# Attention scores of two heads as 64-row products on alternating halves of the array, in a fused attention, routing, experts and dense kernel

## The chip, the cores and the metric

The kernel runs on one core of one Trainium2 chip. The metric is the device time of one execution in microseconds (us). A core has TensorE (PE; its weight loads have their own row, PEld), VectorE (DVE), ScalarE (ACT), GpSimd (POOL) and SyncE (SP), which here only issues transfers. Each engine works through its own queue in order, and they wait for one another by semaphores.

## The reference

Three layers in float32. First attention, with 4 batches, 8 heads, 576 positions and 64 channels a head, in which each row keeps only the scores within `tau` of its largest:

```python
scores = scale * np.matmul(q, k.transpose(0, 1, 3, 2))
thresh = np.max(scores, axis=-1, keepdims=True) - tau
scores = np.where(scores >= thresh, scores, -1000000000.0)
scores = scores - np.max(scores, axis=-1, keepdims=True)
attn = np.exp(scores)
attn = attn / (np.sum(attn, axis=-1, keepdims=True) + 1e-09)
return np.matmul(attn, v).astype(np.float32)
```

Its output is laid out as 2304 tokens of 512 channels. Second, a gate with noise picks two of eight experts for each token, and the token's row becomes the weighted sum of the two experts' outputs (512 to 1024, ReLU, back to 512). Third, a dense layer 512 to 2048 with a slope `alpha` for negative values, and back to 512. `w_in` and `w_out` come as float64 words.

## The kernel before, in words

The order of all instructions is written out by hand; nothing reorders them within an engine.

Products that need float32 accuracy are made of float32r parts: a value is copied to float32r (hi, on ScalarE), and the rest (lo) is a subtraction on GpSimd or VectorE. For attention, a pair of heads is loaded by two transfers into raw tiles of a ring of five (`load_part`, L261): queries as 64 rows (channels) by 2 x 576 columns, keys as 128 rows by 1216 columns, in which rows 64 to 127 repeat rows 0 to 63 and the second head's last 64 keys stand twice. `split_hi` (L277, ScalarE) and `split_lo` (L285, GpSimd) put the queries' hi on rows 0 to 63 and their lo on rows 64 to 127, so that one product with 128 rows sums hi and lo of the queries; it is made once with the keys' hi and once with their lo. Sixteen pairs go through six sets of tiles (`NSET`).

The attention loop (L731) runs over 80 units. A unit is one pair of heads for one tile of 128 rows, or, for the last 64 rows of each head (marked "t"), both heads in one tile. 64 units are of the first kind. The first 16 are the four tiles of each of the first four pairs; after that come 8 "t" units, 32 of the first kind, 8 "t", 16 of the first kind. For a unit and each of its heads: `s_mm` (L334) makes the scores, 4 products of 288 columns into a tile of PSUM (`ps_s`, two of them); `d1` (L355, VectorE) negates and scales them into SBUF and takes the row minimum; `d1b` (L365, VectorE) adds `tau`; `a1` (L369, ScalarE) takes the exponential; `d2` (L381, VectorE) masks by the threshold and sums the row. Then `t_mm` (L394) transposes the result in three parts into `ps_t` (three buffers), `a2` (L409) copies each to SBUF on ScalarE, `pv` (L423) multiplies with the values into `ps_v`. In iteration i the scores are those of unit i, the masks those of unit i-1, the transposes those of i-2, the products with the values those of i-3.

When a tile's four pairs are through, the routing of its tokens follows in pieces set into later iterations (`x_stages`, `gating`): transposes back to token rows with a store (`rows`, one `ps_t`), gate logits (`logits`, one), their transpose (`flip`, one), the sum over heads on VectorE (`sum_`), and for groups of up to three tiles the choice of experts and an indirect store into the experts' slots `xg`. Token rows use a ring of five buffers, one of which holds zeros first: `zero_init` (L684) writes them over all 640 slots of each expert in iterations 9, 11, ... 23. From iteration 64 the first expert's weights are split as well (L173 on GpSimd), and from the end of the loop on PE works on the experts and the last layer.

SyncE issues nearly all transfers, in program order, and waits at each for the buffer it needs.

Of the kernel before, what the change touches and what calls it, by code (L numbers as in the profile page):

```python
# [5 lines left out]
FR = mybir.dt.float32r  # L6
# [16 lines left out]
KW = S + 640  # L23
# [9 lines left out]
def emit(tc, qt, kt, v, tau, wg, wn, noise, w1, w2, w_in, w_out, alpha, out):  # L33
    """qt [B,HP,64,2*S] and kt [B,HP,64,KW]: head pairs, channels on rows; the second
    head's keys lie as tail, main, tail. v [B,S,H*D]. noise [128,NT,E], alpha [128,16]."""
# [6 lines left out]
    with (  # L42
# [10 lines left out]
        # Memory is cut by hand: what the experts and the last layer need takes the place of  # L53
        # attention's tiles piece by piece, as each of them is done with.
# [101 lines left out]
        # the first block runs while attention drains, in other places  # L156
# [35 lines left out]
        def mm1(ps, n, wc, x, col):  # L192
            """wc: the chunks of the four row blocks; columns from col."""
# [33 lines left out]
        # ======================= attention and routing =======================  # L227
# [30 lines left out]

        raw_tile = Ring([cut(m_early, KW * i, [KW]) for i in range(5)])

        def load_part(n, part):  # L261
            b, hp = divmod(n, HP)
            raw = raw_tile()
            raws[n, part] = raw
            if part == "q":
# [4 lines left out]
        def pair(n):  # L270
            t = m_pair[n % NSET]
            return [cut(t, 0, [2, S], FR), cut(t, 3584, [4, 64], FR), cut(t, 1152, [KW], FR), cut(t, 2368, [KW], FR)]

        for i in range(NSET):
            pool.memset(f32(pair(i)[1][:, 1:3]), 0.0)

        def split_hi(n, part):  # L277
            raw = raws[n, part]
            sets[n] = pair(n)
            if part == "q":  # L280
                act.copy(sets[n][0][:64].rearrange("p h s -> p (h s)"), raw[:64, :2 * S])
            else:
                act.copy(sets[n][2], raw)

        def split_lo(n, part, eng):  # L285
            raw = raws.pop((n, part))
            if part == "q":
                a, zt = sets[n][:2]
                af = a.rearrange("p h s -> p (h s)")
                eng.tensor_tensor(af[64:], raw[:64, :2 * S], f32(af[:64]), op=OP.subtract)  # L290
                t0 = TAIL if (n // HP) % 2 == 0 else 0
                for h in range(2):
                    eng.tensor_scalar(zt[:, 3 * h], f32(a[:, h, t0:t0 + 64]), 1.0, 1.0, op0=OP.mult, op1=OP.mult)
            else:
                eng.tensor_tensor(sets[n][3], raw, f32(sets[n][2]), op=OP.subtract)  # L295

        def split_part(n, part, eng):
            split_hi(n, part)
            split_lo(n, part, eng)
# [20 lines left out]
        # The first tiles of rows go side by side: the head pairs come in slower than they are used.  # L320
# [10 lines left out]
        def s_mm(i, h):  # L331
            b, c, hp = units[i]
            a, zt, hi, lo = sets[b * HP + hp]
            u = st[i]  # L334
            ps = psum_s()
            u["ps", h] = ps
            heads = [h] if c != "t" else [0, 1]
            for x in range(2):
                k = 0
                for hh in heads:  # L340
# [755 lines left out]
```

## Time and profile before

| | |
|---|---|
| runs, us | 1294.23, 1295.03, 1299.9; median 1295.03 |
| profiled execution, span in us | 1295.7 |
| mean granted TensorE clock in it | 0.978 |
| busy in it | PE 1200.5 us (93%), PEld 1074.6, DVE 668.7, ACT 551.1, POOL 528.8 |
| moved by DMA | 148.34 MB, mean 114 GB/s |

The prediction quotes five views. The *page* groups instructions: line, engine, operation, output<-input, shapes and count, then busy time in us and mean ns of one, then idle time of the engine just before them and what ended it; its list of transfers has line, queue, count and KB each. *Windows* give each engine's busy time with the number of instructions in a stretch, then the granted clock (1.00 is full), the share of time that the DMA engines were busy, and the GB/s moved. The *chain of waits* is the sequence of work that ended last, with start and length in us. The *timeline* has start, length, engine, line, operation and count, with idle time before it in brackets. The view of one *line* has the shortest, median and longest duration in ns, then the first and last start. A matmul's end is modelled and matmuls overlap, so what n in a row take in all says more than n durations.

### The profile page before, as it was taken

To read this page: it belongs to the slowest core of one execution; us is meant where nothing else is said; L and a number is where in the kernel's file an instruction comes from. 1 tells how busy PE (TensorE), PEld (TensorE's weight loads), DVE (VectorE), ACT (ScalarE), POOL (GpSimd) and SP (SyncE) were. 2 spreads that over 40 slices of the span, in tenths; PEclk is the share of its full clock that TensorE was granted. 3 is DMA by queue.
4 is the path that set the end of the run, shared out by engine and by line. 5 is a ranking of instruction groups with operands and counts; after the bars stand their busy time and mean duration, and the time that the engine had idled before them with its cause. 6 is when DMAs were issued, how large, how long until landed. Compare 5 with 4: busy or idle time off the path is not lost.

```text
span 1295.7 us, 21188 instructions
## 1 busy us (share of the span) xinstructions
PE 1200.5 (93%) x8198; PEld 1074.6 (83%) x8198; DVE 668.7 (52%) x1493; ACT 551.1 (43%) x1029; POOL 528.8 (41%) x529
## 2 busy tenths in 40 slices
PE   4787778989888999999999999999999999999996
PEld 4676667878777889899898989899989988998995
DVE  5795679997996333333343533345424423432440
ACT  4674557766773344434444444443212212221220
POOL 3534245356434244444454454438314413432430
PEclk9898989999999999999999999999999999999998
DMA  4245542231414365555455556552101101111100
GB/s 125 67 144 202 195 145 80 85 123 73 130 59 143 127 202 179 183 180 183 175 198 185 181 166 207 181 187 90 35 31 41 42 17 41 42 33 33 42 9 18
DMA packets 63559, 148.34 MB, mean 114 GB/s; under 512 B 9502, under 2 KB 9886, under 8 KB 63454
## 3 DMA queue, kind: packets, MB, share of 16 engines
q1 hardware_dynamic: 57534, 127.75, 30.0%
q0 software_dynamic: 5760, 18.88, 4.4%
q8 instruction: 66, 1.08, 0.3%
q10 hardware_dynamic: 160, 0.31, 0.1%
q14 instruction: 39, 0.32, 0.1%
HBM read 98.68 MB, written 48.23 MB: 113 GB/s over the span
## 4 chain that ended last, share of the span: by engine, by line
PE 74%; DVE 12%; DMA 6%; issue 2%; POOL 2%; ACT 1%; SPq 1%; DVEq 0%; POOLq 0%; ACTq 0%
PE ps_t L197 33%; PE ps_s L215 32%; DMA m_early<-in_kt_dram 5%; DVE m_hh L386 4%; DVE m_tmp L362 3%; DVE sm L367 2%; PE ps_t L403 2%; PE ps_s L349 2%; PE ps_v L438 1%; DMA xg<-m_gate 1%; PE ps_t L186 1%; POOL m_pair L295 1%; PE ps_v L186 1%; PE ps_s L197 1%; DVE m_gate L481 1%
## 5 line engine op out<-in xcount | busy, mean ns | idle before, releaser
L215 PE MATMUL ps_s<-m_pair,m_hh 128*128 128x512 f32 x1032 | 338.4, 395 | 0.0
L197 PE MATMUL ps_t<-m_v,m_pair 128*128 128x256 f32 (+1 forms) x2016 | 290.6, 295 | 0.0
L197 PEld LDWEIGHTS ps_t<-m_v,m_pair 128*128 128x128 f32 x2016 | 275.7, 191 | 1.4 <-DVE m_v L190 0.3
L215 PEld LDWEIGHTS ps_s<-m_pair,m_hh 128*128 128x128 f32 x1032 | 193.9, 188 | 39.9
L967 POOL TENSOR_TENSOR m_gate<-m_tmp,m_hh 128x256 fp32r<-128x256 f32 x144 | 104.8, 739 | 249.3 <-ACT m_hh L966 248.2
L215 PE MATMUL ps_s<-m_pair,m_gate 128*128 128x512 f32 x516 | 201.6, 391 | 0.0
L173 POOL TENSOR_TENSOR m_pair<-m_v,m_pair 128x1024 fp32r<-128x1024 f32 x55 | 134.7, 2450 | 140.5 <-ACT m_pair L170 136.9
L197 PE MATMUL ps_t<-m_v,m_early 128*128 128x256 f32 (+1 forms) x1152 | 174.9, 296 | 1.3 <-ACT m_v L189 0.8
L197 PEld LDWEIGHTS ps_t<-m_v,m_early 128*128 128x128 f32 x1152 | 161.7, 191 | 3.0 <-ACT m_v L189 1.1
L386 DVE SCALAR_TENSOR_TENSOR m_hh<-m_tmp,sm,m_hh 128x576 f32<-128x576 f32 x144 | 146.4, 1047 | 27.1 <-ACT m_hh L373 26.9
L373 ACT ACTIVATE m_hh<-m_tmp,sm 128x576 f32<-128x576 f32 x144 | 112.3, 781 | 67.3 <-DVE m_tmp L362 66.9
L208 DVE SCALAR_TENSOR_TENSOR m_gate<-ps_t,m_hh 128x384 fp32r<-128x384 f32 (+1 forms) x120 | 58.2, 492 | 153.4 <-ACT m_hh L207 153.4
L403 PE MATMUL ps_t<-ident,m_hh 128*128 128x128 f32 x576 | 93.1, 286 | 47.0 <-DVE m_hh L386 20.9
L349 PE MATMUL ps_s<-m_pair 128*128 128x288 f32 x640 | 126.2, 325 | 8.2 <-ACT m_pair L642 6.6
L963 DVE TENSOR_SCALAR m_tmp<-ps_t,alpha_t 128x256 f32<-128x256 f32 x144 | 69.7, 484 | 117.1 <-PE ps_t L197 117.0
L966 ACT CAST m_hh<-m_tmp 128x256 fp32r<-128x256 f32 x144 | 58.2, 406 | 146.5 <-DVE m_tmp L964 146.4
L403 PEld LDWEIGHTS ps_t<-ident,m_hh 128*128 128x128 f32 x576 | 68.3, 145 | 60.5 <-ACT m_hh L373 18.9
L362 DVE TENSOR_SCALAR_CACHE_REDUCE m_tmp<-ps_s 128x576 f32<-128x576 f32 x144 | 108.2, 751 | 11.0 <-PE ps_s L349 9.8
L215 PEld LDWEIGHTS ps_s<-m_pair,m_gate 128*128 128x128 f32 x516 | 97.1, 188 | 18.1
L349 PEld LDWEIGHTS ps_s<-m_pair 128*128 128x128 f32 x640 | 95.5, 200 | 9.0 <-ACT m_pair L642 6.5
L207 ACT ACTIVATE m_hh<-ps_t 128x384 fp32r<-128x384 f32 (+1 forms) x120 | 52.0, 439 | 93.8 <-PE ps_t L197 92.7
L854 POOL TENSOR_TENSOR m_tmp<-m_tmp 128x512 f32<-128x512 f32 x32 | 41.4, 1292 | 77.8 <-DVE m_tmp L851 74.4
(204 smaller groups left out, 1529.1 us busy)
## 6 DMA issues: line engine op xcount, KB each, us to landing
m_v<-in_w_dram SPq DMA_DIRECT2D x64, 512.0 KB
xg<-m_gate SPq DMA_DIRECT2D x8, 1280.0 KB
yg<-m_tmp SPq DMA_DIRECT2D x40, 256.0 KB
m_early<-in_kt_dram SPq DMA_DIRECT2D x15, 608.0 KB
m_tmp<-in_w_in_dram SPq DMA_DIRECT2D x16, 512.0 KB
m_tmp<-in_w_out_dram SPq DMA_DIRECT2D x16, 512.0 KB
m_v<-xg SPq DMA_DIRECT2D x20, 256.0 KB
m_rows<-xg SPq DMA_DIRECT2D x20, 256.0 KB
```

What stands on the lines that cost most here:

```text
L173: eng.tensor_tensor(WL[n], wraw.pop(n), f32(WH[n]), op=OP.subtract)
L197: pe.matmul(ps[:, :n], w[wc[d]][:, col:col + 128], x[xx][:, d, :n], start=(k == 0), stop=(k == 11))
L208: dve.scalar_tensor_tensor(hs[1][:, f * n:f * n + n], ps, 0.0, f32(h), op0=OP.max, op1=OP.subtract)
L215: pe.matmul(ps, a[:, o:o + 128], ww[w][:, c:c + 512], start=(f == 0 and k == 0), stop=(f == nf - 1 and k == 2))
L349: pe.matmul(ps[:, x, :288], lhs, kk[:, o + x * 288:o + x * 288 + 288], start=(k == 0), stop=(k == 2 * len(heads) - 1))
L362: dve.tensor_scalar(u["sp"][:, h].rearrange("p (a b) -> p a b", a=2), ps[:, :, :288], -0.125, None, op0=OP.mult, op1=OP.min, accum_out=u[" ...
L373: act.activation(u["em"][:, h], u["sp"][:, h], AF.Exp, bias=u["sm"][:, h:h + 1], scale=-1.0)
L386: dve.scalar_tensor_tensor(u["em"][:, h], u["sp"][:, h], sm[:, 2 + h:3 + h], u["em"][:, h], op0=OP.is_le, op1=OP.mult, accum_out=acc)
L403: pe.transpose(ps[:, j * 128:j * 128 + 128], emf[:, o + j * 128:o + j * 128 + 128], ident)
L963: dve.tensor_scalar(t_, ps, 0.0, alpha_t[:, f:f + 1], op0=OP.min, op1=OP.mult)
L966: act.copy(h, g_)
L967: pool.tensor_tensor(hl[:, f * 256:f * 256 + 256], g_, f32(h), op=OP.subtract)
```

## The change

The layout that the host makes is another: queries and keys of a pair come as 128 rows, the first head's channels on rows 0 to 63 and the second's on rows 64 to 127, with 576 columns of queries and 640 of keys (the last 64 keys of both heads stand twice, in front and at the end). Hi and lo are separate tiles, split once on 128 rows; the subtraction on GpSimd is in two pieces. The raw tiles are nine, and pairs 2 and 3 are requested before the routing constants.

The scores of a head are the products hi x hi, hi x lo and lo x hi, each on the head's 64 rows of the array, the two heads in turn, each into its own `ps_s`. The product lo x lo, which before was part of the sum, is left out. For "t" units the queries stand in tiles with zeros in the off-diagonal blocks, and the three products have 128 rows. `thresh` does on ScalarE what `d1b` did on VectorE. `zero_init` writes only the last 128 of an expert's 640 slots. In an iteration, the scores of both heads, both minima, both exponentials and the threshold now stand in front, then the masks, then the transposes.

```diff
--- before.py
+++ after.py
-KW = S + 640
+KW = S + S - TAIL
...
-        raw_tile = Ring([cut(m_early, KW * i, [KW]) for i in range(5)])
+        raw_tile = Ring([cut(m_early, KW * i, [KW]) for i in range(9)])
 
         def load_part(n, part):
             b, hp = divmod(n, HP)
             raw = raw_tile()
             raws[n, part] = raw
+            sp.dma_start(raw[:, :S] if part == "q" else raw, (qt if part == "q" else kt)[b, hp])
+
+        def pair(n):
+            c = Cuts(m_pair[n % NSET])
+            return [c([S], FR), c([S], FR), c([KW], FR), c([KW], FR), c([128], FR), c([128], FR)]
...
+        def tail_tile(n):
+            t = sets[n]
+            t0 = TAIL if (n // HP) % 2 == 0 else 0
+            for k in range(2):
+                for h in range(2):
+                    r = slice(h * 64, h * 64 + 64)
+                    pool.tensor_scalar(t[4 + k][r, r], f32(t[k][r, t0:t0 + 64]), 1.0, 1.0, op0=OP.mult, op1=OP.mult)
+
+        def split_hi(n, part):
+            if n not in sets:
+                sets[n] = pair(n)
             if part == "q":
-                sp.dma_start(raw[:64, :2 * S], qt[b, hp])
+                act.copy(sets[n][0], raws[n, part][:, :S])
             else:
-                sp.dma_start(raw, kt[b, hp][None].to_broadcast([2, 64, KW]))
...
+                act.copy(sets[n][2], raws[n, part])
+
+        def split_lo(n, part):
+            raw = raws.pop((n, part))
+            hi, lo = sets[n][:2] if part == "q" else sets[n][2:4]
+            w = S if part == "q" else KW
+            for o in range(0, w, w // 2):
+                c = slice(o, o + w // 2)
+                pool.tensor_tensor(lo[:, c], raw[:, c], f32(hi[:, c]), op=OP.subtract)
             if part == "q":
...
+                tail_tile(n)
...
-        def s_mm(i, h):
+        def s_mm(i):
             b, c, hp = units[i]
-            a, zt, hi, lo = sets[b * HP + hp]
+            qh, ql, kh, kl, zh, zl = sets[b * HP + hp]
             u = st[i]
-            ps = psum_s()
-            u["ps", h] = ps
...
+            for h in range(nh(i)):
+                u["ps", h] = psum_s()
+            q0 = 0 if c == "t" else c * 128 + (64 if b % 2 else 0)
             for x in range(2):
...
+                for k, (q, z, kk) in enumerate(((qh, zh, kh), (qh, zh, kl), (ql, zl, kh))):
+                    for h in range(nh(i)):
+                        r = slice(0, 128) if c == "t" else slice(h * 64, h * 64 + 64)
+                        lhs = z if c == "t" else q[r, q0:q0 + 128]
+                        o = (64 - 64 * h) + x * 288
+                        pe.matmul(u["ps", h][:, x, :288], lhs, kk[r, o:o + 288], start=(k == 0), stop=(k == 2))
...
-        def d1b(i):
+        def thresh(i):
             sm, n = st[i]["sm"], nh(i)
-            dve.tensor_scalar(sm[:, 2:2 + n], sm[:, 0:n], taut, None, op0=OP.add)
+            act.activation(sm[:, 2:2 + n], sm[:, 0:n], AF.Identity, bias=taut)
...
+        for n in (2, 3):
+            load_part(n, "q")
+            load_part(n, "k")
...
-        loads = [(n, p) for _, n, p, _ in sched[5:]]
+        loads = [(n, p) for _, n, p, _ in sched[6:]]
...
         def zero_init(e):
-            sp.dma_start(xg[e * N:e * N + CAP].rearrange("(t p) d -> p t d", p=128),
-                         zero[:, None, :].to_broadcast([128, CAP // 128, DM]))
+            sp.dma_start(xg[e * N + CAP - 128:e * N + CAP], zero)
...
         for i in range(END):
             it = i - DT
             tiles = 0 <= it < NU
+            if i < NU:
+                s_mm(i)
+                for h in range(nh(i)):
+                    d1(i, h)
+                for h in range(nh(i)):
+                    a1(i, h)
+                thresh(i)
+            else:
+                do_fill()
+            if 0 < i <= NU:
+                for h in range(nh(i - 1)):
+                    d2(i - 1, h)
             if tiles:
                 t_mm(it, 0)
                 a2(it, 0)
-            if 0 < i <= NU:
-                if nh(i - 1) == 2:
-                    a1(i - 1, 1)
-                else:
-                    d2(i - 1, 0)
-            if i < NU:
-                s_mm(i, 0)
-                d1(i, 0)
-            else:
-                do_fill()
             for f, a in at.pop((i, 0), []):
                 f(*a)
             if tiles and nh(it) == 2:
                 t_mm(it, 1)
                 a2(it, 1)
-            if 0 < i <= NU and nh(i - 1) == 2:
-                for h in range(2):
-                    d2(i - 1, h)
-            if i < NU:
-                a1(i, 0)
             iv = it - 1
...
-            if i < NU and nh(i) == 2:
-                s_mm(i, 1)
-                d1(i, 1)
-            elif i >= NU:
+            if i >= NU:
                 do_fill()
-            if i < NU:
-                d1b(i)
             for f, a in at.pop((i, 1), []):
                 f(*a)
```

The order moves on every engine. On PE, around the routing piece that makes gate logits (L489 before, L485 in the change), in the middle of the loop; ps_s are scores, ps_t transposes, ps_v products with the values. Before:

```order
L489 MATMUL ps_t<-m_last,m_rows 32x128 x4
L403 MATMUL ps_t<-ident,m_hh 128x128 x4
L349 MATMUL ps_s<-m_pair_74 128x288 x4
L403 MATMUL ps_t<-ident,m_hh 128x128 x4
L438 MATMUL ps_v<-m_tmp,m_v_77 64x128 x8
L440 MATMUL ps_v<-m_tmp,m_v_77 128x128
L405 MATMUL ps_t<-ident,m_hh 128x128
L349 MATMUL ps_s<-m_pair_74 128x288 x4
L496 MATMUL ps_t<-ident,m_rows 128x128
```

In the change, with the logits in the first row:

```order
L485 MATMUL ps_t<-m_tmp,m_rows 32x128 x4
L347 MATMUL ps_s<-m_pair_74 128x288 x12
L399 MATMUL ps_t<-ident,m_hh 128x128 x8
L434 MATMUL ps_v<-m_tmp,m_v_77 64x128 x8
L436 MATMUL ps_v<-m_tmp,m_v_77 128x128
L401 MATMUL ps_t<-ident,m_hh 128x128
L492 MATMUL ps_t<-ident,m_rows 128x128
L347 MATMUL ps_s<-m_pair_75 128x288 x12
```

The two groups of 4 products, which stood before and after the transposes, are one group of 12, and both groups of transposes follow it directly; the routing piece stands last in a unit, behind the third transposes, and right in front of the next scores.

On ScalarE around the copy of such logits (L492 before, L488 in the change; L373 and L369 are the exponentials, L415/L417 and L411/L413 the copies of transposes). Before:

```order
L415 COPY m_tmp<-ps_t 128x512
L373 ACTIVATE m_hh<-m_tmp,sm_133 128x576
L415 COPY m_tmp<-ps_t 128x512
L373 ACTIVATE m_hh<-m_tmp,sm_126 128x576
L417 COPY m_tmp<-ps_t 128x128
L283 CAST m_pair_76<-m_early 128x1216
L492 COPY m_rows<-ps_t 128x128
L415 COPY m_last<-ps_t 128x512
L373 ACTIVATE m_hh<-m_tmp,sm_126 128x576
L415 COPY m_last<-ps_t 128x512
L373 ACTIVATE m_hh<-m_tmp,sm_127 128x576
```

In the change:

```order
L369 ACTIVATE m_hh<-m_tmp,sm_144 128x576 x2
L363 ACTIVATE sm_144<-sm_144,taut 128x2
L411 COPY m_tmp<-ps_t 128x512 x2
L413 COPY m_tmp<-ps_t 128x128
L291 CAST m_pair_76<-m_early 128x640
L488 COPY m_rows<-ps_t 128x128
L369 ACTIVATE m_hh<-m_tmp,sm_145 128x576 x2
L363 ACTIVATE sm_145<-sm_145,taut 128x2
L411 COPY m_last<-ps_t 128x512 x2
L413 COPY m_last<-ps_t 128x128
```

Exponentials and copies took turns; now both exponentials and the threshold (L363) of unit i stand ahead of all copies of unit i-2. The split copies (L281, L283; L291 in the change) keep their place at the end of an iteration, with half the columns.

More of the change, by code (lines that the diff above doesn't have):

```diff
@@ L264, in load_part @@
             raws[n, part] = raw
+            sp.dma_start(raw[:, :S] if part == "q" else raw, (qt if part == "q" else kt)[b, hp])
+        def pair(n):
+            c = Cuts(m_pair[n % NSET])
+            return [c([S], FR), c([S], FR), c([KW], FR), c([KW], FR), c([128], FR), c([128], FR)]
+        for i in range(NSET):
+            for z in pair(i)[4:]:
+                for h in range(2):
+                    pool.memset(f32(z[h * 64:h * 64 + 64, 64 - h * 64:128 - h * 64]), 0.0)
+        def tail_tile(n):
+            t = sets[n]
+            t0 = TAIL if (n // HP) % 2 == 0 else 0
+            for k in range(2):
+                for h in range(2):
+                    r = slice(h * 64, h * 64 + 64)
+                    pool.tensor_scalar(t[4 + k][r, r], f32(t[k][r, t0:t0 + 64]), 1.0, 1.0, op0=OP.mult, op1=OP.mult)
@@ L619, in emit @@
         qr, kr = raw_tile(), raw_tile()
[L620 to L629 removed]
+        first = [(qt[0, 0], qr, sets[0][0], sets[0][1], 0, 256), (kt[0, 0], kr, sets[0][2], sets[0][3], 0, 352),
+                 (kt[0, 0], kr, sets[0][2], sets[0][3], 352, KW), (qt[0, 0], qr, sets[0][0], sets[0][1], 256, S)]
+        for i, (src, dst, _, _, c0, c1) in enumerate(first):
+            (sp, act)[i % 2].dma_start(dst[:, c0:c1], src[:, c0:c1])
         sp.dma_start(taut, bass.AP(tensor=tau.tensor, offset=tau.offset, ap=[[0, 128], [1, 1]]))
@@ L633, in emit @@
         load_v(0)
-        load_part(2, "q")
-        qa, zt0, khi, klo = sets[0]
-        for i, (c0, c1) in enumerate(((0, 256), (0, S), (S, KW), (256, S))):
-            if i in (0, 3):
-                act.copy(qa[:64, :, c0:c1], qv[:64, :, c0:c1])
-                (dve if i == 0 else pool).tensor_tensor(qa[64:, :, c0:c1], qv[:64, :, c0:c1], f32(qa[:64, :, c0:c1]),
-                                                        op=OP.subtract)
-            else:
-                act.copy(khi[:, c0:c1], kr[:, c0:c1])
-                dve.tensor_tensor(klo[:, c0:c1], kr[:, c0:c1], f32(khi[:, c0:c1]), op=OP.subtract)
-        for h in range(2):
-            pool.tensor_scalar(zt0[:, 3 * h], f32(qa[:, h, TAIL:]), 1.0, 1.0, op0=OP.mult, op1=OP.mult)
-        load_part(2, "k")
-        load_part(3, "q")
+        for n in (2, 3):
+            load_part(n, "q")
+            load_part(n, "k")
+        for i, (_, raw, hi, lo, c0, c1) in enumerate(first):
+            act.copy(hi[:, c0:c1], raw[:, c0:c1])
+            (dve if i < 3 else pool).tensor_tensor(lo[:, c0:c1], raw[:, c0:c1], f32(hi[:, c0:c1]), op=OP.subtract)
+        tail_tile(0)
         zero = xtok_ring()
@@ L675, in do_lo @@
         def do_lo(n, p, eng):
-            split_lo(n, p, eng)
+            split_lo(n, p)
             next_load()
```

55 lines of the change are left out of this document (3 added, 52 removed).

## Prediction

> **What bounds the kernel now.** I read the windows by stage first, cut at the times at which units 0, 16, 24, 56, 64 and 79 of the attention loop took their threshold (line 367; a unit is one pair of heads for one tile of 128 rows).
>
> ```profile
> core 0: us, PE busy (x) PEld busy (x) DVE busy (x) ACT busy (x) POOL busy (x), PEclk, DMA share, GB/s
> 0.00:10.20 10.20, 3.46 (x12) 2.90 (x12) 3.80 (x7) 4.95 (x7) 5.49 (x27) 1.00 0.70 190
> 10.20:93.90 83.70, 62.33 (x517) 53.60 (x517) 67.71 (x143) 53.18 (x101) 33.64 (x22) 0.96 0.30 98
> 93.90:134.20 40.30, 31.73 (x249) 27.68 (x248) 24.47 (x58) 18.93 (x38) 15.33 (x24) 0.87 0.56 201
> 134.20:294.00 159.80, 128.57 (x1230) 109.72 (x1229) 139.97 (x369) 104.73 (x198) 68.16 (x88) 0.94 0.36 126
> 294.00:323.50 29.50, 27.51 (x229) 24.23 (x228) 21.68 (x64) 17.98 (x38) 20.64 (x38) 1.00 0.17 60
> 323.50:392.50 69.00, 59.77 (x562) 51.21 (x561) 65.65 (x169) 49.70 (x94) 25.58 (x31) 0.98 0.28 89
> 450.00:1295.70 845.70, 834.58 (x5059) 758.20 (x5057) 319.36 (x599) 281.39 (x515) 341.90 (x278) 0.99 0.34 111
> ```
>
> From 450 us on PE is busy 834.58 of 845.70 us with the experts and the last layer, which the change leaves alone: whatever attention gains or loses moves that block as a whole. Attention's 80 units take the first 395 us, 4.9 us each. No engine is full there, so I read the chain of waits next.
>
> ```profile
> 18.96 20.09 DMA m_early<-in_kt_dram
> 39.12 16.55 DMA m_early<-in_kt_dram
> 95.84 22.74 DMA m_early<-in_kt_dram
> 150.66 15.29 DMA xg<-m_gate
> m_early<-in_kt_dram SPq DMA_DIRECT2D x15, 608.0 KB
> m_early<-in_qt_dram SPq DMA_DIRECT2D x15, 288.0 KB
> xg<-m_gate SPq DMA_DIRECT2D x8, 1280.0 KB
> ```
>
> Three stretches wait for a pair's keys. The fourth waits for zeros: the zero tile is one of the five row buffers, and the fifth tile of rows may not be written into it before all eight zeroing transfers (10.5 MB together) have read it. Where nothing is awaited from a DMA, VectorE meets GpSimd:
>
> ```profile
> 67.02 0.81 DVE L386 SCALAR_TENSOR_TENSOR m_hh<-m_tmp,sm,m_hh 128x576 f32<-128x576 f32 x1
> 69.98 2.79 POOL L295 TENSOR_TENSOR m_pair<-m_early,m_pair 128x1216 fp32r<-128x1216 f32 x1 [6.13 <-ACT m_pair L283]
> 70.28 3.10 DVE L386 SCALAR_TENSOR_TENSOR m_hh<-m_tmp,sm,m_hh 128x576 f32<-128x576 f32 x1
> L367 DVE TENSOR_SCALAR sm<-sm,taut 128x2 f32<-128x2 f32 x45 | 31.1, 690 | 1.6
> L290 POOL TENSOR_TENSOR m_pair<-m_early,m_pair 64x1152 fp32r<-64x1152 f32 x12 | 32.3, 2690 | 24.9 <-issue 17.3 <-PE ps_t L403 5.6 <-POOL m_pair L295 0.9
> ```
>
> The mask (L386) takes 0.81 us alone and 3.10 us when a split runs on GpSimd; it ends with the split. The row of L367 is out of the groups by shape between 60 and 340 us, where its mean, 690 ns for two columns, is the same wait.
>
> Undisturbed, a unit is limited by PE, whose loads in one unit are these (the first two rows give the shortest, median and longest of all loads and products of scores):
>
> ```profile
> L349 PEld LDWEIGHTS ps_s<-m_pair x640: 186/189/338, 6.5 to 391.3; 128*128 128x128 f32 x160
> L349 PE MATMUL ps_s<-m_pair x640: 289/296/607, 6.6 to 391.4; 128*128 128x288 f32 x160
> 238.17 0.49 PEld L403 LDWEIGHTS ps_t<-ident,m_hh 128*128 128x128 f32 x4
> 238.83 0.85 PEld L438 LDWEIGHTS ps_v<-m_last,m_v 128*64 128x64 f32 x16 [0.17 <-issue]
> 238.83 1.09 PE L438 MATMUL ps_v<-m_last,m_v 128*64 128x128 f32 x16
> 239.85 0.30 PEld L440 LDWEIGHTS ps_v<-m_last,m_v 128*128 128x128 f32 x2 [0.17 <-issue]
> 240.07 0.14 PEld L405 LDWEIGHTS ps_t<-ident,m_hh 128*128 128x128 f32 x1
> 240.18 0.57 PEld L349 LDWEIGHTS ps_s<-m_pair 128*128 128x128 f32 x4
> 240.91 0.16 PEld L489 LDWEIGHTS ps_t<-m_last,m_rows 128*32 128x32 f32 x8 [0.16 <-issue]
> ```
>
> Transposes 2 x 0.49, values 0.85 + 0.22 with 0.17 of idle before each (the array changes from full to column halves and back), the last transpose 0.11: 2.50 us. The scores are two bursts of 4; loads of 0.19 come 0.13 apart ((0.57 - 0.19)/3), so 8 take 1.04. Together 3.54, with the routing's pieces (0.3 a unit) 3.84.
>
> **The change, part by part.** *Keys, queries and zeros by DMA.* Keys fall from 608 to 320 KB a pair (128 rows of 640 columns), and a zeroing transfer from 1280 to 256 KB, so zeros from 10.5 to 2.1 MB. With nine raw tiles, pairs 2 and 3 are also asked for ahead of the routing constants. Up to pair 3 the start needs 4 x 608 KB and 1.28 MB of values, 3.7 MB, which at 98 to 190 GB/s (the first two stages) is there by 20 to 38 us; pair 3 is split at units 6 and 7, some 35 us in. The waits of 20.09, 16.55 and 22.74 us should thus be short ones. For what the 1.28 MB of values still take from pair 1 I leave 6 us. The wait of 15.29 us should vanish: 2.1 MB at 201 GB/s are 10 us, spread over 15 units.
>
> *Splits.* GpSimd's subtractions become pieces of 288 and 320 columns: 2690 x 288/1152 = 0.67 us and 2.79 x 320/1216 = 0.73 us. VectorE then waits at most some 0.7 us behind one instead of 2.3, and has that much slack (below). ScalarE copies half as many columns.
>
> *Scores.* Twelve products of 64 rows replace eight of 128, in six pairs on the two halves of the rows. No row of before shows two row halves at once. The nearest shows column halves: L438's sixteen take 1.09 us, (1.09 - 0.27)/15 = 55 ns each, while full ones that stream as many columns (L433) take (1.05 - 0.28)/7 = 110 ns:
>
> ```profile
> L438 PE MATMUL ps_v<-m_tmp,m_v x512: 272/273/476, 28.6 to 401.0; 128*64 128x128 f32 x171
> 305.66 1.05 PE L433 MATMUL ps_v<-m_last,m_v 128*128 128x128 f32 x8
> 306.64 0.29 PEld L434 LDWEIGHTS ps_v<-m_last,m_v 64*128 64x128 f32 x2
> 309.21 1.05 PE L433 MATMUL ps_v<-m_tmp,m_v 128*128 128x128 f32 x8
> 240.91 0.43 PE L489 MATMUL ps_t<-m_last,m_rows 128*32 128x128 f32 x8
> ```
>
> L489, on quarters, takes 8 in 0.43 us. So parts of the array load and multiply side by side. Bounds for the burst: 6 x 0.13 = 0.78 us if row halves do the same, 12 x 0.13 = 1.56 us if not. I take 0.78, being nearest to L438, whose order alternates halves just as the new loop does. Each entry into row halves and each exit should cost idle time like the 0.17 to 0.20 around L438 and L489; I take 0.2 twice a unit. PE's sum becomes 0.78 + 0.4 + 2.50 = 3.68, plus 0.3 of routing 3.98. The Trainium skill ("TensorE: Matmul & The Clock Gate", Part 3, The mechanism) says that loads for another row group overlap running products and that products on different row groups run at once; no row here shows it for rows.
> A second rule there speaks against the change (Part 2, LDWEIGHTS): a load's time goes by its columns, not its rows, 107 ns for 128. By it twelve loads in line would be an estimated 1.28 us, and the trace agrees on the columns: two 64-row loads (L434) take 0.29 us, two of 128 rows (L440) 0.30.
>
> *Threshold.* It leaves VectorE (0.69 us on average) for ScalarE, where the nearest row is a small activation (L526; the first row is for the sum below):
>
> ```profile
> L173 POOL TENSOR_TENSOR m_pair<-m_v,m_pair 128x1024 fp32r<-128x1024 f32 x55 | 134.7, 2450 | 140.5 <-ACT m_pair L170 136.9
> L526 ACT ACTIVATE m_gate<-m_rows 128x24 f32<-128x24 f32 x5 | 1.2, 231 | 0.0
> 239.13 0.75 DVE L362 TENSOR_SCALAR_CACHE_REDUCE m_tmp<-ps_s 128x576 f32<-128x576 f32 x1
> 239.81 0.08 DVE L362 DVE_READ_ACCUMULATOR m_tmp<-ps_s 128x1 f32 x1
> 239.92 0.78 ACT L373 ACTIVATE m_hh<-m_tmp,sm 128x576 f32<-128x576 f32 x1 [0.16 <-DVE m_tmp L362]
> 243.17 0.57 ACT L415 COPY m_last<-ps_t 128x512 f32<-128x512 f32 x1
> ```
>
> 0.2 us, and it waits for both heads' minima. Queued behind it are the copies of the transposes (L415), and here the new order bites.
>
> *Order.* Both heads' scores come first in a unit; on ScalarE both exponentials and the threshold stand ahead of the copies. A unit in the routing stages allocates four transpose buffers out of three, so its routing piece waits for the copy of the same unit's first transposes. From the first score load: scores end at 0.03 + 5 x 0.13 + 0.30, about 1.0; the two minima, 0.76 each (0.68 to the read of the sum and 0.08), at 2.5; the second exponential, 0.78, at 3.3; threshold 0.2, 3.5; copy 0.57, 4.1; routing piece 0.13 to 0.49, change of array 0.2: the next scores start at about 4.6. Where the piece is the flipped logits, its reader on VectorE stands behind both masks (2.5 + 2 x 0.81 = 4.1) and holds the next unit's last transpose about as long. So 4.6 us per unit, 0.6 beyond PE's 3.98, where before's 32 units of the fourth stage took (159.8 - 15.3)/32 = 4.5. VectorE's minima and masks need 2 x 0.76 + 2 x 0.81 = 3.1 of that; over 1 us is left for routing and for a split of 0.7.
>
> *The sum.* First unit: 10.2 becomes 9.7 by smaller first pieces. Units 0 to 15 have no routing piece: PE's 3.68, rounded up to 3.85 for ScalarE's splits in between, x 16 + 6 = 67.6 against 83.7: -16.1. Eight tail units: the two L433 rows above stand 3.55 apart, less two products of 0.13: 3.3 x 8 = 26.4 against 40.3, -13.9. Thirty-two units at 4.6: 147.2 against 159.8, -12.6. Eight tails: 26.4 against 29.5, -3.1. Fifteen units at 4.6, and 3 us for the first expert's weight splits (L173, 2.45 us each on GpSimd, as before): 72 against 69, +3. With -0.5 in front: -43.2. 1295.7 - 43.2 = 1252.5; that span lies 0.7 above the median of the runs, so 1252.
>
> **The rivals.** (A) The copy comes soon enough, PE sets the pace throughout: 47 units x (4.6 - 3.98) = 29 us more, 1223. For it: my chain adds seven small steps, each rounded up. Against: four buffers out of three.
> (B) Slower: the row halves run one after the other. Price 0.78 us x 64 units = 50 us, 1302, as the score burst is on the chain that sets 4.6. From a burst of 1.45 us on (0.78 + 43/64) nothing is gained. For it: no row shows row halves at work together. Against: L438 and L489.
> (C) Products overlap, loads go in line: twelve loads at the 0.11 us of L440's two (0.30 - 0.19), 1.32 us, + 0.54 x 64 = 35: 1287. This is what the skill's rule on loads would do. Against: L489's eight loads in 0.16 us.
> (D) The waits for keys go only as their bytes: pair 1 to 3 arrive with the values, as 20.09 and 16.55 suggest, and a third of the bytes is saved (896 to 608 KB): the second stage gains 5 instead of 16, the third some 8 less: 1271. For it: 98 GB/s in that stage, under half of 201.
>
> **How the numbers follow.** Forecast 52%, A 14%, B 10%, C 11%, D 13%. The range 1222 to 1292 takes in A, C and D and leaves B out, with part of the forecast's own spread of 1238 to 1266. A measurement tells 0.5%, 6.5 us, from no change: under 1288.5 lie the forecast, A, D and just over half of C, 85%; B lies at the upper bound, 1301.5, and I give 8 of its 10% to slower; 7% is left between.
>
> **What would show it.** The new scores' matmuls: starts in pairs a few ns apart and bursts near 0.8 us (else B or C). Idle of 0.2 before the scores' loads and after. Units 24 to 55 at 4.6 us with PE waiting for the copies of transposes (else A). No wait above 6 us for keys, none for zeros (else D). The mask's mean near 0.8 us. Wrong altogether would be an experts' stage that isn't 846 us long, or that starts late for its weights.

## The result and the profile after

The changed kernel takes 1245.39 us (median of four runs, 1245.06 to 1247.19) against 1295.3 us before: the ratio is 0.960, with a 95% interval of 0.958 to 0.962. The span of its profiled execution is 1245.1 us. Its windows, cut as those of before at the thresholds of units 0, 16, 24, 56, 64 and 79, and for the last row 845.70 us ahead of the end, the length of that row before:

```profile
core 0: us, PE busy (x) PEld busy (x) DVE busy (x) ACT busy (x) POOL busy (x), PEclk, DMA share, GB/s
0.00:8.80 8.80, 3.43 (x19) 2.49 (x21) 2.72 (x7) 4.24 (x8) 7.12 (x43) 1.00 0.73 234
8.80:65.50 56.70, 55.64 (x564) 44.84 (x564) 52.91 (x125) 49.25 (x114) 30.06 (x46) 1.00 0.44 131
65.50:93.50 28.00, 27.40 (x246) 23.37 (x242) 18.16 (x49) 18.57 (x49) 12.12 (x30) 1.00 0.35 112
93.50:238.50 145.00, 127.11 (x1341) 99.60 (x1342) 114.28 (x339) 101.10 (x228) 57.34 (x114) 1.00 0.25 86
238.50:265.70 27.20, 25.77 (x231) 22.28 (x225) 17.42 (x57) 18.81 (x48) 15.62 (x39) 1.00 0.19 71
265.70:338.20 72.50, 62.70 (x621) 49.52 (x620) 59.04 (x154) 51.30 (x109) 25.71 (x34) 0.95 0.23 85
338.20:399.40 61.20, 55.51 (x380) 49.70 (x379) 28.35 (x97) 21.49 (x49) 22.25 (x27) 0.97 0.40 142
399.40:1245.10 845.70, 831.59 (x5044) 755.75 (x5042) 318.04 (x597) 280.58 (x513) 340.51 (x277) 1.00 0.33 110
```

In the last row PE is busy 831.59 us, where it was 834.58. From the first expert's long run of products on (L215, under "The end of the loop" below) the kernel before takes 878.4 us and the changed one 880.0, so all that was won was won ahead of it. The table sets the stages beside those of before and the forecast, and beside three of the experiments below (stage lengths in us, from the starts of the same six thresholds in each trace).

| stage | before | forecast | after | e10 | e4 | e12 |
|---|---|---|---|---|---|---|
| to the first threshold | 10.2 | 9.7 | 8.8 | 10.9 | 8.7 | 10.2 |
| units 0 to 15 | 83.7 | 67.6 | 56.7 | 71.0 | 57.2 | 65.8 |
| 8 tail units | 40.3 | 26.4 | 28.0 | 30.0 | 27.0 | 33.6 |
| 32 units with routing | 159.8 | 147.2 | 145.0 | 147.8 | 134.7 | 170.3 |
| 8 tail units | 29.5 | 26.4 | 27.2 | 28.6 | 26.7 | 32.3 |
| 15 units | 69.0 | 72 | 72.5 | 68.5 | 65.6 | 80.1 |
| last threshold at | 392.5 | 349.3 | 338.2 | 356.8 | 319.9 | 392.3 |

In the waits of after up to 350 us, PE, VectorE and ScalarE wait for a transfer only once, 1.5 us for the first queries:

```profile
ACT m_pair L628 <- DMA m_early<-in_qt_dram: 1.5, 1, 1.5
ACT m_hh L369 <- DVE m_tmp L358: 89.4, 70, 3.9
PEld ps_t L401 <- ACT m_tmp L411: 9.4, 13, 0.7
PEld ps_t L485 <- ACT m_tmp L411: 7.4, 9, 2.1
PEld ps_t L492 <- ACT m_last L411: 5.9, 9, 0.7
PEld ps_t L475 <- ACT m_last L411: 5.6, 9, 1.1
```

(Columns: total us, times, longest.) The three waits of 16 to 23 us for keys are gone, and so is the one for zeros. What PE still waits for in the last four rows are copies of the transposes (L411), 28.3 us in all. One unit with routing in the timeline of after, from the routing piece of the unit ahead of it to its own third transposes:

```profile
190.54 0.14 PEld L492 LDWEIGHTS ps_t<-ident,m_rows 128*128 128x128 f32 x1 [0.66 <-ACT m_last L411]
190.80 0.82 PEld L347 LDWEIGHTS ps_s<-m_pair 64*128 64x128 f32 x12
191.78 0.86 PEld L399 LDWEIGHTS ps_t<-ident,m_hh 128*128 128x128 f32 x8 [0.16 <-issue]
191.89 0.76 DVE L358 TENSOR_SCALAR_CACHE_REDUCE m_tmp<-ps_s 128x576 f32<-128x576 f32 x1 [1.39 <-PE ps_s L347]
192.69 1.45 ACT L369 ACTIVATE m_hh<-m_tmp,sm 128x576 f32<-128x576 f32 x2 [1.55 <-DVE m_tmp L358]
192.80 0.85 PEld L434 LDWEIGHTS ps_v<-m_last,m_v 128*64 128x64 f32 x16 [0.17 <-issue]
194.05 0.28 ACT L363 ACTIVATE sm<-sm,taut 128x2 f32<-128x2 f32 x1
194.24 1.05 ACT L411 COPY m_tmp<-ps_t 128x512 f32<-128x512 f32 x2
194.85 0.14 PEld L401 LDWEIGHTS ps_t<-ident,m_hh 128*128 128x128 f32 x1 [0.72 <-ACT m_tmp L411]
```

The next scores' loads start at 195.11, 4.31 us after these. ScalarE waits 1.55 us for the first minimum (L358), then makes both exponentials and the threshold; only then comes the copy (L411), which the third transposes (L401) await for 0.72 us. Twelve loads of 64 rows take 0.82 us.

### The profile page after: what moved, and what is told of

It is laid out like the page before. It is cut to its first block, busy times and chain, and to the rows that moved or that the text cites. A ratio compares the mean times of both kernels' runs of the same rounds, so it can differ in the third digit from the quotient of the medians.

```text
span 1245.1 us, 21730 instructions
## 1 busy us (share of the span) xinstructions
PE 1189.1 (96%) x8422; PEld 1047.5 (84%) x8422; DVE 610.9 (49%) x1413; ACT 545.3 (44%) x1109; POOL 510.7 (41%) x609
## 4 chain that ended last, share of the span: by engine, by line
PE 83%; ACT 5%; DVE 5%; issue 4%; POOL 1%; DMA 1%; SPq 0%; ACTq 0%; DVEq 0%; POOLq 0%
PE ps_t L197 33%; PE ps_s L215 33%; PE ps_s L347 6%; PE ps_t L399 2%; ACT m_hh L369 2%; DVE m_tmp L358 2%; PE ps_v L434 2%; DVE m_hh L382 1%; PE ps_t L186 1%; ACT sm L363 1%; ACT m_tmp L411 1%; PE ps_v L436 1%; PE ps_v L186 1%; ACT m_last L411 1%; PE ps_t L475 1%
## 5 line engine op out<-in xcount | busy, mean ns | idle before, releaser
L215 PE MATMUL ps_s<-m_pair,m_hh 128*128 128x512 f32 x1032 | 338.4, 395 | 0.0
L215 PEld LDWEIGHTS ps_s<-m_pair,m_hh 128*128 128x128 f32 x1032 | 193.9, 188 | 39.9
L215 PE MATMUL ps_s<-m_pair,m_gate 128*128 128x512 f32 x516 | 201.7, 391 | 0.0
L369 ACT ACTIVATE m_hh<-m_tmp,sm 128x576 f32<-128x576 f32 x144 | 105.4, 774 | 89.6 <-DVE m_tmp L358 89.4
L382 DVE SCALAR_TENSOR_TENSOR m_hh<-m_tmp,sm,m_hh 128x576 f32<-128x576 f32 x144 | 133.2, 957 | 0.0
L358 DVE TENSOR_SCALAR_CACHE_REDUCE m_tmp<-ps_s 128x576 f32<-128x576 f32 x144 | 103.9, 754 | 58.8 <-PE ps_s L347 58.3
L215 PEld LDWEIGHTS ps_s<-m_pair,m_gate 128*128 128x128 f32 x516 | 97.1, 188 | 18.3 <-DVE m_gate L208 0.2
L347 PE MATMUL ps_s<-m_pair 64*128 64x288 f32 (+1 forms) x864 | 90.2, 321 | 7.1 <-ACT m_pair L628 4.4
L347 PEld LDWEIGHTS ps_s<-m_pair 64*128 64x128 f32 (+1 forms) x864 | 70.2, 195 | 19.4 <-issue 5.6
L399 PE MATMUL ps_t<-ident,m_hh 128*128 128x128 f32 x576 | 82.7, 284 | 1.1 <-ACT m_last L411 0.4
L299 POOL TENSOR_TENSOR m_pair<-m_early,m_pair 128x288 fp32r<-128x288 f32 (+1 forms) x60 | 54.5, 929 | 59.1 <-ACT m_pair L289 37.7
L399 PEld LDWEIGHTS ps_t<-ident,m_hh 128*128 128x128 f32 x576 | 64.4, 143 | 12.8 <-issue 7.4
```

What stands on the lines that cost most here:

```text
L215: pe.matmul(ps, a[:, o:o + 128], ww[w][:, c:c + 512], start=(f == 0 and k == 0), stop=(f == nf - 1 and k == 2))
L347: pe.matmul(u["ps", h][:, x, :288], lhs, kk[r, o:o + 288], start=(k == 0), stop=(k == 2))
L358: dve.tensor_scalar(u["sp"][:, h].rearrange("p (a b) -> p a b", a=2), ps[:, :, :288], -0.125, None, op0=OP.mult, op1=OP.min, accum_out=u[" ...
L369: act.activation(u["em"][:, h], u["sp"][:, h], AF.Exp, bias=u["sm"][:, h:h + 1], scale=-1.0)
L382: dve.scalar_tensor_tensor(u["em"][:, h], u["sp"][:, h], sm[:, 2 + h:3 + h], u["em"][:, h], op0=OP.is_le, op1=OP.mult, accum_out=acc)
L399: pe.transpose(ps[:, j * 128:j * 128 + 128], emf[:, o + j * 128:o + j * 128 + 128], ident)
```

## The experiments

Each kernel is the kernel before or the changed one with the edit shown; ratios are against the kernel before, with their 95% intervals.

### What held the keys up

The change makes keys smaller, asks for two pairs earlier, and fetches each pair's keys without a repeated source. Two experiments give the first two back, one at a time.

**e5** adds to the changed kernel, behind each pair's keys, a copy of 288 KB into memory that nobody reads.

```diff
             sp.dma_start(raw[:, :S] if part == "q" else raw, (qt if part == "q" else kt)[b, hp])
+            if part == "k":
+                sp.dma_start(spare[n], kt[b, hp][:, :S])
```

> The changed kernel, with a further transfer of 288 KB behind each pair's keys, copied into memory that nobody reads, so that a pair moves as many bytes as before (896 KB). Theory (what removed the key waits is that requests stand further ahead, and the bytes have room): 0 to +4 us, 1243 to 1250, mostly in the first 25 us. Rival (the waits went with their bytes): key waits of 5 us and more come back, +8 to +20, 1253 to 1266.

1245.73 us, ratio 0.960 (0.958 to 0.963). **e6** goes back to a ring of five raw tiles and to the old order of requests.

```diff
-        raw_tile = Ring([cut(m_early, KW * i, [KW]) for i in range(9)])
+        raw_tile = Ring([cut(m_early, KW * i, [KW]) for i in range(5)])
...
-        for n in (2, 3):
-            load_part(n, "q")
-            load_part(n, "k")
+        load_part(2, "q")
...
         tail_tile(0)
+        load_part(2, "k")
+        load_part(3, "q")
...
-        loads = [(n, p) for _, n, p, _ in sched[6:]]
+        loads = [(n, p) for _, n, p, _ in sched[5:]]
```

> The changed kernel with five raw tiles instead of nine, and the requests where they stood before: pair 2's keys and all of pair 3 after the first splits, each later part one request further behind. Theory (being asked for early is what counts): the requests of pair 2's keys and pair 3 stand behind the values and the routing constants again, and waits come back, +10 to +25 us, 1255 to 1270. Rival (half the bytes alone remove the waits): 1243 to 1249.

1244.74 us, ratio 0.960 (0.957 to 0.963). Neither costs anything that can be measured, so in the changed kernel neither the bytes nor the early requests carry the gain. What was left is the form of the transfer. In the kernel before, the windows between the issue of pair 2's keys (18.96 us) and their landing, and the timeline of the copy that waits for them:

```profile
19.00:39.00 20.00, 12.61 (x102) 10.75 (x102) 12.58 (x27) 10.17 (x19) 6.79 (x4) 1.00 0.27 79
39.08 1.21 ACT L283 CAST m_pair<-m_early 128x1216 fp32r<-128x1216 f32 x1 [3.98 <-DMA m_early<-in_kt_dram]
```

608 KB (622,592 bytes) in the 20.09 us from issue to landing that the chain showed are 31 GB/s, while the sixteen DMA engines are busy 27% of the time (the row ends with clock, DMA share and GB/s). The transfer wasn't short of bandwidth; it didn't use it. In the packet records of that trace its packets, 4864 bytes each, are under way only from 25.97 to 38.70 us, 12.7 us (49 GB/s); until 22.17 us those of pair 1's keys were, which have the same form. So 7.0 of the 20.09 us pass before its first packet, part of them behind pair 1's keys. Over the 15 pairs the packets of one pair's keys take 13.9 us (median), and never more than 4 are under way at once, where packets of other large transfers reach 14 to 22.

**e10** makes in the kernel before, of that one transfer with a repeating source, two plain ones of 64 rows, with the same bytes to the same places.

```diff
-                sp.dma_start(raw, kt[b, hp][None].to_broadcast([2, 64, KW]))
+                for k in range(2):
+                    sp.dma_start(raw[k * 64:k * 64 + 64], kt[b, hp])
```

> The kernel before (1295.7 us), with a pair's keys fetched as two plain transfers of 64 rows instead of one that repeats its source over both halves; bytes, requests and everything else as before. New theory (neither bytes nor lateness of the request made keys late, but the form: 608 KB asked for at 18.96 us land at 39.05, 31 GB/s, with the DMA engines 27% busy): keys land within 5 to 8 us, the waits of 20.1, 16.6 and part of 22.7 us shrink; units 0 to 16 come down from 83.7 to about 66 us (3.2 and 5.1 us in turn), stage three by 5 to 10: 1266 to 1277. Rival (bytes or the place of the request): 1290 to 1300.

1258.23 us, ratio 0.969 (0.966 to 0.972): one line gives 3.1 of the change's 4.0%, more than either theory allowed. The page of e10 and the windows of its units 0 to 15:

```profile
m_early<-in_kt_dram SPq DMA_DIRECT2D x30, 304.0 KB, 3.9
xg<-m_gate SPq DMA_DIRECT2D x8, 1280.0 KB, 7.0
10.94:81.94 71.00, 58.15 (x517) 50.95 (x517) 68.12 (x141) 53.46 (x101) 34.09 (x21) 1.00 0.64 185
```

Half a pair's keys land in 3.9 us, and the stage moves 185 GB/s where before moved 98. The packets of a pair's keys now take 3.0 us (median), with up to 20 under way at once. The Trainium skill has the rule ("DMA: Bandwidth & Descriptors", in the section on why a DMA increments its semaphore by 16, and again in its rules for authors): the outermost dimension of both sides sets how many of the sixteen engines a transfer uses, and a leading repeat of c copies confines it to at most c. Here c is 2. The at most 4 packets under way, the 13.9 us and e10 agree with it; no record names the engine of a packet.

**The zeros.** **e3** takes over only the shorter zeroing into the kernel before.

```diff
-            sp.dma_start(xg[e * N:e * N + CAP].rearrange("(t p) d -> p t d", p=128),
-                         zero[:, None, :].to_broadcast([128, CAP // 128, DM]))
+            sp.dma_start(xg[e * N + CAP - 128:e * N + CAP], zero)
```

> The kernel before (1295.3 us) with only the last 128 of an expert's 640 slots zeroed, nothing else. Theory: the wait of 15.3 us for zeros and most of the wait of 22.7 us for keys at 95.8 us go, and 5 us of GpSimd contention come out in their place: 1262 to 1272. Rival (the keys at 95.8 us are late by their own bytes): only the 15.3 us go, 1278 to 1283.

1275.43 us, ratio 0.984 (0.982 to 0.986): some 20 us won, between the two expectations. In stages cut as above, the first tails take 34.1 us instead of 40.3, the 32 routing units 147.2 instead of 159.8. Its chain still holds the waits for keys, one of them longer than before:

```profile
19.14 19.70 DMA m_early<-in_kt_dram
65.11 29.63 DMA m_early<-in_kt_dram
94.80 17.80 DMA m_early<-in_kt_dram
```

So the zeros look like a cause of their own, worth 20 us. **e2** gives all zeros back to the changed kernel (the reverse of that edit), and **e11** takes e3's edit and e10's together.

> The changed kernel with all 640 slots of an expert zeroed again (10.5 MB instead of 2.1). Theory (zeros cost before by the row buffer they hold, 15.3 us of wait, and by standing in the keys' way, 22.7 us): in the changed kernel keys are asked for three parts further ahead, and the fifth tile of rows is due at about 110 us, while 10.5 MB from 42 us on at 180 GB/s end at about 100 us; so little comes back, 0 to +8 us: 1245 to 1253. Rival (the wait for zeros is the same wherever they stand): +15 or more, 1260 to 1275.

> The kernel before with both: plain key transfers and only 128 slots an expert zeroed. Theory (the change's gain is mostly these two, as its units of the routing stages take as long as before's): no wait for a DMA over 5 us is left in attention; 1248 to 1260. Rival (scores, shorter splits and the new order bring a good part of the 50 us): 1262 to 1276.

e2: 1246.66 us, ratio 0.961 (0.959 to 0.963), no change. e11: 1259.43 us, ratio 0.971 (0.968 to 0.973), the same as e10. Once the keys are plain, 10.5 MB of zeros cost nothing that can be measured: in e10 each zeroing transfer lands in 7.0 us. The 32 routing units, which held the wait of 15.29 us for zeros, take 147.8 us in e10 with all zeros in place and 147.2 in e3 with slow keys in place: either edit alone takes that wait away, so their gains are not a sum. The 20 us of e3 exist only beside the slow keys.

### Whether the halves of the array work together

**e1** makes all three products of one head before those of the other, so that in the queue three products on the same half stand in a row.

```diff
-                for k, (q, z, kk) in enumerate(((qh, zh, kh), (qh, zh, kl), (ql, zl, kh))):
-                    for h in range(nh(i)):
+                for h in range(nh(i)):
+                    for k, (q, z, kk) in enumerate(((qh, zh, kh), (qh, zh, kl), (ql, zl, kh))):
```

> The changed kernel (1245.4 us), with the three products of one head before the three of the other in each half of the columns, so that neighbours in the queue stand mostly on the same 64 rows. Theory (row halves work side by side only where neighbours alternate): the twelve loads, 0.82 us in the changed kernel, take between 9 x 0.13 = 1.17 us (three changes of head still overlap) and 12 x 0.13 = 1.56 us; as the burst is on the chain that sets a unit, 64 x 0.35 to 0.74 us more: 1268 to 1293 us. Rival (the loads and products of both halves would overlap in any order, or the burst is hidden): bursts of 0.8 us and 1243 to 1248.

1246.11 us, ratio 0.961 (0.959 to 0.963). The burst in the timeline of e1:

```profile
195.07 0.82 PEld L347 LDWEIGHTS ps_s<-m_pair 64*128 64x128 f32 x12
```

It is as short as with the heads in turn. The theory that the alternation makes the overlap fell. The loads' records show the same: they start in pairs some 10 ns apart, although three of one half are queued ahead of the other's first; with alternation the pairs start mostly 3 or 4 ns apart. (A record doesn't name its half; that a pair is one load of each is read from the length of the burst.) The order within this burst doesn't matter.

**e12** asks what the burst is worth: the changed kernel makes each product of scores twice and halves the scale, so the scores are the same and the burst is twice as long.

```diff
-                for k, (q, z, kk) in enumerate(((qh, zh, kh), (qh, zh, kl), (ql, zl, kh))):
+                for k, (q, z, kk) in enumerate(((qh, zh, kh), (qh, zh, kl), (ql, zl, kh)) * 2):
...
-                        pe.matmul(u["ps", h][:, x, :288], lhs, kk[r, o:o + 288], start=(k == 0), stop=(k == 2))
+                        pe.matmul(u["ps", h][:, x, :288], lhs, kk[r, o:o + 288], start=(k == 0), stop=(k == 5))
...
-                              -0.125, None, op0=OP.mult, op1=OP.min, accum_out=u["sm"][:, h:h + 1])
+                              -0.0625, None, op0=OP.mult, op1=OP.min, accum_out=u["sm"][:, h:h + 1])
```

> The changed kernel with every score product made twice and the scale halved, so that the scores are the same: a burst of 24 in place of 12 (12 for 6 in the tail units). It measures what a burst as long as that of halves in turn would cost. Theory (the burst is on the chain that sets a unit, in all stages): 0.78 us x 80 units = 62 us more, 1300 to 1312. Rival (much of it disappears in PE's idle time of the routing stages, 0.4 to 0.7 us a unit): only the first 16 units and the tails pay in full, 1270 to 1285.

1300.4 us, ratio 1.002 (1.001 to 1.004). In its timeline:

```profile
197.48 1.62 PEld L347 LDWEIGHTS ps_s<-m_pair 64*128 64x128 f32 x24 [0.20 <-issue]
```

The burst is 0.80 us longer, and the kernel 55 us, 0.69 us for each of 80 units; in the 32 routing units it is (170.3 - 145.0)/32 = 0.79, the whole burst. So the scores are on the chain there, and halves that worked one after the other would have left nothing of the change's gain.

### VectorE, GpSimd and the order

**e8** cuts only GpSimd's subtractions of the kernel before into four pieces each.

```diff
-                eng.tensor_tensor(af[64:], raw[:64, :2 * S], f32(af[:64]), op=OP.subtract)
+                for o in range(0, 2 * S, 288):
+                    c = slice(o, o + 288)
+                    eng.tensor_tensor(af[64:, c], raw[:64, c], f32(af[:64, c]), op=OP.subtract)
...
-                eng.tensor_tensor(sets[n][3], raw, f32(sets[n][2]), op=OP.subtract)
+                for o in range(0, KW, 304):
+                    c = slice(o, o + 304)
+                    eng.tensor_tensor(sets[n][3][:, c], raw[:, c], f32(sets[n][2][:, c]), op=OP.subtract)
```

> The kernel before (1295.7 us) with GpSimd's subtractions in four pieces of 288 or 304 columns; nothing else, so GpSimd has as much to do. Theory (VectorE waits for the end of one GpSimd instruction, up to 2.3 us, and gets in between two): a mask or threshold waits some 0.5 us instead of 2, but may meet a second piece; 30 splits x 1 us on the way, 15 to 30 us less: 1265 to 1281. Rival (VectorE then waits at every piece, as GpSimd's work is the same): 1290 to 1300.

1288.13 us, ratio 0.994 (0.992 to 0.996): a gain, under the theory's. The groups by shape between 60 and 340 us:

```profile
L390 DVE SCALAR_TENSOR_TENSOR m_hh<-m_tmp,sm,m_hh 128x576 f32<-128x576 f32 x108 | 95.3, 913 | 22.3 <-ACT m_hh L377 22.1
L371 DVE TENSOR_SCALAR sm<-sm,taut 128x2 f32<-128x2 f32 x46 | 20.8, 453 | 1.6
L299 POOL TENSOR_TENSOR m_pair<-m_early,m_pair 128x304 fp32r<-128x304 f32 x50 | 49.6, 1023 | 23.8 <-ACT m_pair L283 23.5
```

The mask (here L390) falls from 1032 ns in the same window of before to 913, the threshold (L371) from 690 to 453. But a quarter of the columns takes 1.02 us on GpSimd instead of a quarter of 2.79, and VectorE still meets one piece after another.

**e9** moves only the threshold of the kernel before to ScalarE, **e7** moves it back to VectorE in the changed kernel (the reverse edit).

```diff
-            dve.tensor_scalar(sm[:, 2:2 + n], sm[:, 0:n], taut, None, op0=OP.add)
+            act.activation(sm[:, 2:2 + n], sm[:, 0:n], AF.Identity, bias=taut)
```

> The kernel before (1295.7 us) with the threshold added on ScalarE (0.28 us each in the changed kernel) instead of VectorE; nothing else. Theory (what the threshold pays behind a split is paid by the next mask instead): only its own 0.23 us on VectorE go, in the units that VectorE sets: 0 to 12 us less, 1283 to 1297. Rival (the threshold's waits, 31 us between 60 and 340 us, go with it): 1262 to 1275.

> The changed kernel with the threshold added on VectorE again, behind the two minima. Theory (in the routing stages the threshold on ScalarE, 0.2 us from its start to the next copy's, stands in front of the copy that sets a unit): 47 units x 0.2 = 9 us less, up to 4 us of it lost to waits behind splits: 1235 to 1242. Rival (VectorE's 0.23 us or its waits decide): 1246 to 1258.

e9: 1301.6 us, ratio 1.003 (1.002 to 1.005), somewhat slower. Its masks between 60 and 340 us:

```profile
L386 DVE SCALAR_TENSOR_TENSOR m_hh<-m_tmp,sm,m_hh 128x576 f32<-128x576 f32 x102 | 113.6, 1132 | 37.2 <-ACT sm L367 23.0 <-ACT m_hh L373 13.7
```

The mask now waits 23.0 us for the threshold and itself takes 1132 ns instead of 1032: the time that the small addition spent behind GpSimd went to the mask. e7: 1246.31 us, ratio 0.961 (0.958 to 0.963), no change; the theory's 9 us didn't come. Its stages differ from those of after by at most 0.7 us, although single undisturbed units are shorter (4.13 us, scores at 187.54 to scores at 191.67, against 4.31). Where that is lost again the traces didn't settle.

**e4** tests the chain that the forecast set at 4.6 us. The copy of the first transposes goes between the two exponentials, and the routing's first piece ahead of the masks.

```diff
-                for h in range(nh(i)):
-                    a1(i, h)
+                a1(i, 0)
+                if tiles:
+                    t_mm(it, 0)
+                    a2(it, 0)
+                if nh(i) == 2:
+                    a1(i, 1)
                 thresh(i)
+                for f, a in at.pop((i, 0), []):
+                    f(*a)
...
-            if tiles:
+            if tiles and i >= NU:
                 t_mm(it, 0)
                 a2(it, 0)
```

> The changed kernel with another order on ScalarE and VectorE: the copy of the first transposes stands between the two exponentials instead of behind them and the threshold, and the sum of the flipped logits stands ahead of the masks. Theory (in the routing stages a unit's 4.3 to 4.6 us are set by the routing piece's wait for that copy): these units fall to PE's sum, 3.7 to 4.0 us, 47 units x 0.5 = 24 us less: 1218 to 1228. Rival (another engine, VectorE with 114 of 145 us busy, or GpSimd, sets these units): 1240 to 1247.

1224.14 us, ratio 0.944 (0.942 to 0.946), within the theory's 1218 to 1228. It is the fastest kernel here. The timeline of e4 in the routing stage, from the third transposes on:

```profile
150.25 0.14 PEld L401 LDWEIGHTS ps_t<-ident,m_hh 128*128 128x128 f32 x1
150.56 0.82 PEld L347 LDWEIGHTS ps_s<-m_pair 64*128 64x128 f32 x12 [0.17 <-PE ps_v L436]
```

The last transpose waits for nothing, and the scores follow with one change of the array. The 32 routing units fall from 145.0 to 134.7 us, 4.53 to 4.21 each, and the last 15 from 72.5 to 65.6; the stages without routing change by 1 us or less. The waits of L401 and L492 for a copy, 15.3 us in after, are absent from e4's. The 3.7 to 4.0 us a unit of the theory were not quite reached, and the edit moves two things, the copy and the routing's first piece, which were not run apart.

## Why the prediction was right, and where it was wrong

**The time.** 1252 was forecast with a range of 1222 to 1292, 1245 came. Three steps came out at their size (the burst of scores, the change of array, the routing unit's chain); the largest was right for a wrong reason.

**Keys by DMA: the step that failed.** The forecast put the waits of 20.09, 16.55 and 22.74 us down to bytes (896 to 608 KB a pair) and to late requests. e5 and e6 give each back at no cost; e10 shows that the repeating source was the cause, at 3.1 of the 4.0%. The sign was right by luck, because the new layout happens to drop that source. The signs of it were in the rows quoted then: 608 KB in 20.09 us from issue to landing are 31 GB/s, in a stage whose DMA engines were busy 30% of the time, and the chain held keys alone, never the queries of plain form. The prediction divided all bytes by the rate of the whole stage and never a single transfer's by its own time. So the 6 us left for keys and values in units 0 to 15 were not needed. Rival D (waits shrink as bytes) fell with it. The first tails owe most of their gain to the keys as well: 40.3 us before, 30.0 in e10, 28.0 after, 26.4 forecast.

**Units 0 to 15** gained 27.0 us where 16.1 were forecast. Of the 10.9 between, 6 are the wait left for keys that didn't come, 5 are 3.54 us a unit instead of 3.85. From before to e10, by the keys alone, the stage falls by 12.7 us, from e10 to after by 14.3; in that second step VectorE's busy time falls by 15.2, from 68.12 of 71.00 us to 52.91 of 56.70. That VectorE set the pace in e10 is read from these rows; that mostly shorter subtractions freed it is argued from e8, since e7 gives nothing to the threshold. Plain keys with short pieces alone were not run. The granted clock, which the forecast left out, rose in units 0 to 55 from 0.96, 0.87 and 0.94 to 1.00. What that is worth was not separated; in units 0 to 15 e11 takes 71.1 us at 0.93 where e10 takes 71.0 at 1.00.

**Zeros.** The wait vanished as forecast, but the price of the step holds only beside the slow keys (e3 against e2 and e11).

**Splits.** Forecast 0.67 and 0.73 us a piece; the view of their line, shortest, median and longest in ns, and the page's row of the mask:

```profile
L299 POOL TENSOR_TENSOR m_pair<-m_early,m_pair x60: 789/862/1396, 10.6 to 258.6; 128x288 fp32r<-128x288 f32 x30, 128x320 fp32r<-128x320 f32 x30
L382 DVE SCALAR_TENSOR_TENSOR m_hh<-m_tmp,sm,m_hh 128x576 f32<-128x576 f32 x144 | 133.2, 957 | 0.0
```

Mean 0.93 us on the page's account, median 0.86: a piece doesn't shrink as its columns do (in e8, too, 304 take 1.02 us where 1216 take 2.79). The mask's mean is 957 ns against 1047 before, not near 0.8 as the forecast would show it. A wait behind GpSimd has got shorter and has not gone. Nor did the mask in the rows quoted end with the split, as the prediction says: the split ends at 72.77 us and the mask at 73.38, 0.61 us later.

**Scores.** The view of their line after:

```profile
L347 PEld LDWEIGHTS ps_s<-m_pair x864: 182/185/334, 4.4 to 335.1; 64*128 64x128 f32 x154, 128*128 128x128 f32 x19
```

One load takes 0.185 us, twelve take 0.82, so they follow each other by (0.82 - 0.185)/11 = 0.058 us, two in 0.116 against 0.13 forecast: side by side. Rival C, loads in line at 1.32 us, fell with that, and the 0.78 stands. So does the idle at a change of array: 0.16 us behind the scores, ahead of L399, and 0.17 ahead of them where nothing else is awaited (L347 in e4's timeline), 0.2 forecast. The Trainium skill ("TensorEngine Tiling (Array Packing)", Key Properties) says both, that tiles load and multiply in parallel and that a change of tiling mode drains the array; the 0.82 and the 0.16 us agree. Rival B's price, 1302 for halves in turn, is confirmed by e12 at 1300 for a burst of the length that B supposed.

On PE itself the new scores are no shorter: 0.82, 0.16 and 0.17 us make 1.15, where eight products of 128 rows took 1.04; the forecast's own sums, 3.68 against 3.54 us a unit, say as much. What the layout gives is about half the columns to split, and fewer bytes, which were worth nothing by themselves (e5). Scores of 128 rows were not put back into the changed kernel: between e11 (1259.4 us) and it (1245.4) lie 14 us for scores, splits, threshold and order together.

**Threshold.** 0.28 us on ScalarE instead of 0.2. By itself the move is worth nothing (e7) or a little less (e9).

**Order.** 4.6 us a routing unit forecast, 4.53 measured (145.0/32), for the reason given: the copy stands behind both exponentials and the threshold. e4 takes that away and gets 21 us, against the 29 that rival A set for PE as the pace. So A named a real reserve, that this change leaves unused.

**The end of the loop.** 54.3 us were won at the last threshold and 50 in the end. The first expert's long run of 42 products starts in the chains of before and of after at

```profile
417.33 12.40 PE ps_s L215 x42
```

```profile
338.24 0.28 ACT sm L363
365.12 11.10 PE ps_s L215 x42
```

that is 24.8 us behind the last threshold before (392.5) and 26.9 after. Part of that is only where the threshold now stands in a unit; the remaining 1.6 us lie behind. The forecast took this stretch as unchanged.

## What to carry to other kernels

Divide each awaited transfer's bytes by its own time before blaming bandwidth; if it is far under its neighbours' rate while the DMA engines are idle, look at the form of its access pattern, above all a small outermost dimension. Two edits that empty the same queue do not add up, so price each with the other in place as well as alone. When an engine's queue holds work for two stages of a pipeline, put the piece that another engine awaits between the others rather than behind them.

## What the runs showed of the hardware that was not expected

A transfer whose source is a row block repeated twice by its outermost dimension had its packets under way for 13.9 us (median of 15 pairs, 45 GB/s), with at most 4 at once; the same bytes as two plain transfers take 3.0 us (e10, 207 GB/s). It held up what was queued with it: beside plain keys the wait of 15.29 us for zeros is gone too, with the zeros unchanged.

Products on the two row halves of the array overlap even when three of one half stand in the queue ahead of the other half's first (e1): 0.82 us for twelve in either order.

A GpSimd subtraction of 304 columns takes 1.02 us where one of 1216 takes 2.79 (e8): four pieces cost 4.1 us instead of 2.8, and the kernel still gains by them.
